# Cosine attention and highway FFN on one core: k and v on 112 lanes of four tokens, transposes by DMA from batch 2 on, v cast by its load, GpSimd behind VectorE's port

## The chip, the core and the metric

One core of a Trainium2 chip runs the whole kernel. The metric is the device time of one execution in microseconds (us); the time before is the median of 3 runs, 313.31 us (312.57 to 313.74). One further execution was profiled. Engines: PE is TensorE (matmuls; PEld are its weight loads), DVE is VectorE, ACT is ScalarE, POOL is GpSimd, SP is SyncE, which here only issues DMA transfers. POOL issues transfers too, and only its transfers change the type on the way (float32 to float16).

## The reference

Eight batches, 12 heads, 448 tokens, 64 elements a head; the rows of q and k are brought to length one, the scores are scaled by 1/tau = 10, and a highway FFN of 768 columns follows.

```python
q_n = q / (np.linalg.norm(q, axis=-1, keepdims=True) + 1e-06)
k_n = k / (np.linalg.norm(k, axis=-1, keepdims=True) + 1e-06)
scores = np.matmul(q_n, k_n.transpose(0, 1, 3, 2)) / tau
attn = np.exp(scores - np.max(scores, axis=-1, keepdims=True))
out  = np.matmul(attn / (np.sum(attn, axis=-1, keepdims=True) + 1e-09), v)
x = out.transpose(0, 2, 1, 3).reshape(B * S, H * D)
H = np.maximum(x @ w_h, 0.0)
T = 1.0 / (1.0 + np.exp(-(x @ w_t + b_t)))
return T * H + (1.0 - T) * x
```

## The kernel before

The heads of a batch are taken in six pairs (head p with head p + 6); pair number s = 6 b + p runs from 0 to 47. 448 tokens are not a multiple of 128: 384 of them lie on 128 lanes with three tokens each ("main"), and the last 64 are "tails" with tiles of their own. Most work is in float16.

For each batch b: main rows of q and k come by POOL's queue as float16 (`qr`, `kr`), v by SP's as float32 (`vr`), tails by SP's (`qt`, `kt`, `vt`). DVE squares the main rows (L462), ACT the tails (L486); DVE folds the squares in two halvings and a sum (L477 to L479), and seven Newton steps of 24 to 48 elements give the reciprocal roots (L505 to L512). A chain of loads, squares, folds and Newton steps thus precedes a batch; its loads of q, k and v wait for an exponential of pair 6 b - 8 (`GO`). Tails of k are scaled by DVE (`ktnorm`, L558).

For each pair:

- POOL scales q and k by their roots (`scaled`, L531; `qtn` for q's tails, L544).
- `turn`: nine PE transposes (L576 to L584) put q, k and tails into one PSUM bank, and DVE copies it to `qT` (L590, 1024 columns).
- `scores`: six matmuls on half of the rows (L599, two for each of three chunks of 128 keys), one full matmul for the 64 tail keys of both heads (`qkt`, L613); ACT takes the exponentials (L606 for a chunk, L618 for the tails).
- ACT casts v into `vp` (L626, and L634 for the tails; DVE does it in batch 0). `vp` has a column of ones, so that the sums of the exponentials come out of the same product.
- `attend`: 32 matmuls of 65 columns (L647, L650, L666); DVE takes the reciprocal (L680) and scales into `x` (L683).

The FFN of a batch has four groups, three of 128 x 768 and one of tails: x is transposed (by a DMA on SP's queue in batches 1 to 6, L709; by PE in batches 0 and 7, L715), PE multiplies by both weights in halves (L738, L744, L749), ACT takes tanh (L763), DVE ends with L770, L777 and L781, POOL adds (L787) and SP stores (L797, L795).

Every engine takes its instructions in the order of the program. That order comes from a list of operation numbers, `ORDER`, which is written out in the kernel; `Plan.follow` goes along it with a cost for each operation, gives each tile a buffer of its ring, and sorts by the starts so found. Work of the FFN is thus put by hand between that of the pairs on every engine. In the planner an operation with `port=True` (of POOL, and of DVE from SBUF to SBUF) starts only when the one before it of either engine is over; in the program nothing enforced this.

Of the kernel before, what the change touches and what calls it, by code (L numbers as in the profile page):

```python
# [19 lines left out]
9 8 4 0 12 10 7 6 11 14 2 13 5 3 18 15 22 23 24 250 25 28 26 16 17 27 29 249 30 248 31 40 32 33 247 251 34 35  # L20
36 37 39 38 20 64 252 65 66 253 63 67 19 68 41 69 21 42 70 43 78 74 51 79 76 75 44 45 46 52 77 72 47 53 73 48
54 1 49 55 50 56 86 57 58 59 60 87 61 62 90 105 88 71 259 109 82 124 80 89 81 83 143 128 97 91 84 98 166 95
106 92 85 125 147 107 96 93 144 108 126 94 162 116 127 110 117 112 163 101 111 100 99 272 164 113 255 129 135
130 131 145 132 133 146 102 136 103 114 165 134 154 466 464 104 173 115 137 254 463 148 465 139 260 256 152
155 140 261 149 119 118 257 467 120 262 121 258 153 167 138 122 263 174 469 141 150 123 168 264 271 151 468
171 265 273 172 169 266 156 274 158 170 267 157 275 159 268 176 276 269 175 160 270 161 177 283 178 277 179
285 278 288 180 279 284 287 280 142 281 181 307 282 329 289 182 291 326 217 310 290 199 286 306 200 298 292
218 299 296 325 308 293 344 327 309 297 294 345 328 317 295 311 364 336 346 312 301 383 347 300 318 302 303
363 337 313 304 315 367 305 355 382 314 365 235 183 356 366 316 332 184 333 319 322 320 185 330 386 334 331
374 321 186 323 335 324 349 187 375 340 350 341 681 679 488 338 339 348 471 353 680 188 351 682 192 354 195  # L30
189 342 343 352 193 683 190 194 357 191 360 358 685 236 368 196 372 369 359 470 384 684 373 201 197 361 385
370 475 362 389 476 202 472 198 371 393 477 219 473 394 478 474 390 387 378 377 479 379 388 487 391 207 480
392 489 208 481 203 490 502 482 491 398 397 396 483 395 492 602 484 376 493 485 545 494 486 495 503 209 526
564 496 380 204 497 507 399 499 498 400 583 205 501 210 500 206 381 504 211 212 401 523 505 542 506 514 213
508 522 515 512 225 509 541 524 513 220 560 525 510 221 222 579 511 543 214 517 686 518 519 516 215 544 527
691 531 520 528 223 521 598 533 216 552 692 226 534 693 529 687 553 240 530 694 688 228 532 241 695 561 227
229 224 689 536 231 418 535 242 580 537 538 690 237 599 539 696 540 548 550 723 238 697 703 551 562 435 698
230 549 581 563 546 239 402 232 547 243 233 582 571 403 572 699 554 700 404 556 701 555 244 818 234 405 702
245 742 780 565 569 720 246 566 557 408 558 719 559 570 406 409 739 407 567 410 586 738 568 411 600 716 587
575 717 576 574 757 601 573 588 577 584 414 589 590 578 758 609 412 591 715 422 413 452 610 419 895 704 585  # L40
898 721 415 896 593 705 592 897 594 416 722 595 603 607 596 604 597 428 899 423 706 608 707 605 425 417 606
708 429 709 901 710 424 426 711 430 718 612 712 611 427 613 900 761 614 713 714 436 776 615 616 726 728 919
727 740 777 730 741 729 420 795 437 617 731 439 421 796 442 438 902 440 724 431 441 745 432 725 749 759 903
443 750 433 760 734 746 735 444 733 732 908 747 904 434 743 907 453 748 814 736 737 445 744 909 905 764 454
910 765 906 815 754 753 911 455 752 448 934 751 459 446 912 755 913 756 799 762 634 766 447 763 778 914 449
768 767 797 915 450 779 456 769 798 783 939 781 916 784 771 920 451 618 917 782 921 621 918 773 922 1034 772
935 958 770 923 457 954 774 924 800 775 651 802 801 619 458 931 787 925 806 620 926 933 622 788 460 624 936
623 627 803 625 630 461 807 628 626 977 1113 1112 804 927 932 785 805 638 928 629 955 635 786 929 1114 930 631
1111 808 636 791 1115 632 637 790 789 639 792 462 640 810 793 811 794 816 647 937 633 817 973 956 1117 938 974
819 823 957 820 825 946 992 809 1116 652 826 812 1011 813 947 668 641 824 1119 821 642 822 1136 658 643 993  # L50
644 1123 1015 827 1012 828 830 829 645 831 832 940 944 646 941 653 833 1118 655 654 648 945 975 1120 656 1124
649 976 942 657 961 943 965 994 664 661 962 650 1125 659 1121 966 1126 1122 1030 963 959 964 662 1127 1031 660
949 850 960 948 1128 951 663 978 1129 665 950 979 968 1130 969 666 952 1131 970 953 980 982 1132 995 981 967
984 667 1013 971 1133 985 972 672 983 1014 669 1134 1155 1135 673 1193 1148 670 1212 1231 1147 674 989 867 671
986 987 1250 1149 988 1174 834 675 990 1152 996 991 837 1171 997 1001 998 835 676 1151 1003 1032 1002 677 838
1033 1004 999 1190 678 1018 839 840 1000 1137 843 1019 841 1170 1007 842 836 1008 1189 1005 1150 1006 1020 846
1016 1138 1021 1022 1153 1009 1139 1023 844 1010 1017 1037 1329 1327 1154 854 1038 845 1024 1328 851 1140 1330
847 855 1141 848 1142 1143 1025 856 1144 1027 1331 1145 1039 1146 1035 1208 1040 1026 1041 1028 1172 1332 1209
1029 1042 852 1036 849 1173 1228 857 1333 868 853 1227 858 863 1043 884 859 860 1046 1334 861 1045 862 1158
1156 1159 864 1162 1191 865 1163 1044 1192 1160 1157 869 1047 1048 1246 871 866 1161 1049 1247 1175 870 872  # L60
1176 1164 1335 1166 1167 1339 1352 1165 873 874 1168 880 1177 1340 1179 1169 1181 1178 1210 1341 1336 875 1182
1342 1180 1196 1337 877 1343 1338 1200 1197 878 876 1198 1201 1066 1194 1344 1211 1186 1199 1183 1345 1219 879
1195 1185 1346 1215 881 1184 1216 1351 1204 1203 1205 882 1187 1220 1347 1202 1188 1213 1390 1217 1348 1206
1214 1349 888 1207 883 885 1353 1218 889 1350 1354 1428 886 1363 890 1371 1223 1355 1083 887 1050 1368 1409
1447 1356 1222 1357 1051 1367 1366 1358 1359 1224 1360 1056 1361 1052 1365 1221 1364 1053 891 1225 1229 892
1362 1226 893 1054 1230 1057 1386 1055 894 1059 1058 1387 1232 1236 1233 1248 1062 1238 1405 1249 1237 1369
1060 1370 1424 1239 1067 1100 1466 1061 1544 1234 1547 1063 1253 1235 1068 1064 1257 1070 1254 1546 1073 1543
1258 1255 1069 1251 1545 1256 1406 1241 1240 1076 1252 1425 1243 1065 1242 1077 1244 1549 1245 1071 1078 1074
1072 1259 1548 1075 1260 1261 1079 1084 1568 1388 1080 1372 1556 1389 1443 1376 1373 1262 1378 1081 1263 1407
1264 1379 1085 1408 1377 1265 1087 1462 1082 1086 1374 1393 1551 1375 1088 1444 1090 1394 1380 1383 1463 1381  # L70
1089 1391 1395 1096 1392 1382 1550 1397 1426 1384 1398 1567 1091 1396 1093 1385 1555 1092 1412 1101 1413 1557
1569 1399 1582 1094 1427 1402 1282 1400 1095 1401 1570 1416 1414 1403 1417 1571 1104 1415 1102 1097 1105 1572
1558 1103 1098 1573 1559 1410 1106 1299 1606 1431 1435 1574 1432 1404 1445 1099 1266 1575 1107 1436 1576 1108
1272 1446 1411 1109 1269 1577 1644 1578 1552 1110 1419 1587 1421 1625 1270 1553 1663 1273 1554 1271 1418 1682
1267 1274 1560 1420 1268 1561 1433 1562 1429 1422 1563 1434 1423 1454 1464 1564 1278 1455 1286 1565 1465 1430
1450 1566 1287 1581 1451 1440 1579 1438 1437 1288 1439 1580 1452 1448 1583 1441 1453 1442 1283 1602 1275 1449
1284 1621 1276 1285 1584 1458 1277 1316 1456 1457 1459 1279 1469 1460 1603 1471 1470 1461 1585 1280 1473 1586
1472 1604 1289 1605 1474 1640 1588 1281 1467 1589 1292 1659 1290 1468 1295 1590 1291 1622 1300 1591 1475 1641
1607 1609 1608 1476 1660 1478 1594 1477 1610 1301 1479 1480 1595 1611 1592 1612 1293 1303 1294 1481 1593 1306
1296 1302 1304 1297 1597 1305 1596 1599 1598 1613 1312 1298 1623 1600 1614 1601 1307 1678 1624 1617 1309 1308  # L80
1679 1626 1630 1627 1310 1632 1311 1498 1631 1317 1313 1320 1633 1314 1318 1321 1319 1628 1322 1515 1642 1629
1323 1315 1615 1324 1482 1643 1325 1636 1651 1326 1647 1652 1649 1618 1648 1616 1634 1619 1661 1650 1620 1483
1662 1485 1484 1670 1486 1671 1637 1487 1635 1645 1638 1664 1494 1646 1488 1639 1502 1665 1489 1656 1490 1668
# [150 lines left out]
def kernel(  # L234
# [11 lines left out]
    nc = tc.nc  # L246
# [639 lines left out]
```

## Time and profile before

| what | value |
|---|---|
| median of 3 runs | 313.31 us |
| the profiled execution | 313.04 us |
| its span, first to last instruction | 311.2 us |
| DVE busy | 240.4 us (77%) |
| ACT busy | 205.8 us (66%) |
| POOL busy | 160.9 us (52%) |
| share of DMA engines: SP's queue, POOL's queue | 39.6%, 28.5% |
| granted TensorE clock over the span | 0.987 |
| first turn of pair 12, last product of pair 47 | 81.1 us, 282.5 us |

A busy matmul is not a PE at its peak: matmuls are pipelined, so what one costs is read from the distance between the starts of neighbours. Three stages can be told apart: a start of some 50 us, in which loads and the norms of the first batches set the pace; the middle, in which pairs and FFN groups are mixed on PE; and a tail of 28.7 us after the last pair, in which only the FFN is left.

### The profile page before, as it was taken

To read this page: it belongs to the slowest core of one execution; us is meant where nothing else is said; L and a number is where in the kernel's file an instruction comes from. 1 tells how busy PE (TensorE), PEld (TensorE's weight loads), DVE (VectorE), ACT (ScalarE), POOL (GpSimd) and SP (SyncE) were. 2 spreads that over 40 slices of the span, in tenths; PEclk is the share of its full clock that TensorE was granted. 3 is DMA by queue.
4 is the path that set the end of the run, shared out by engine and by line. 5 is a ranking of instruction groups with operands and counts; after the bars stand their busy time and mean duration, and the time that the engine had idled before them with its cause. 6 is when DMAs were issued, how large, how long until landed. Compare 5 with 4: busy or idle time off the path is not lost.

```text
span 311.2 us, 7957 instructions
## 1 busy us (share of the span) xinstructions
PE 264.0 (85%) x3178; PEld 164.1 (53%) x3178; DVE 240.4 (77%) x548; ACT 205.8 (66%) x327; POOL 160.9 (52%) x162
## 2 busy tenths in 40 slices
PE   0148946998699999899988999979899999999992
PEld 0115635665356565457555565645565656666661
DVE  5897796489789896998799887994799845454574
ACT  1445972989485868875776949948688795761210
POOL 9539145612882958259456864268712766112440
PEclk9999995999999999999999999999999999999999
DMA  7999999992212399439972399319985014301313
GB/s 170 225 223 216 229 192 240 142 235 88 26 53 51 103 148 280 96 97 154 284 117 78 54 197 285 91 35 138 243 183 103 15 53 101 103 15 54 128 53 126
DMA packets 79750, 42.21 MB, mean 136 GB/s; under 512 B 60224, under 2 KB 76608, under 8 KB 79712
## 3 DMA queue, kind: packets, MB, share of 16 engines
q1 hardware_dynamic: 53104, 29.60, 39.6%
q0 software_dynamic: 24992, 11.31, 28.5%
q10 hardware_dynamic: 1616, 0.79, 0.9%
q8 instruction: 25, 0.41, 0.6%
q14 instruction: 13, 0.11, 0.1%
HBM read 37.75 MB, written 11.01 MB: 157 GB/s over the span
## 4 chain that ended last, share of the span: by engine, by line
PE 43%; DVE 33%; DMA 15%; issue 4%; POOL 2%; ACT 1%; ACTq 0%; DVEq 0%; POOLq 0%
PE pB L749 16%; DMA qr<-in_q_dram 7%; PE pS L599 6%; PE pB L650 5%; DVE f L477 4%; DMA out_dram<-os 4%; DVE n L479 3%; DVE hm L770 3%; DVE x L683 3%; DVE qT L590 3%; DVE sq L462 3%; DMA kr<-in_k_dram 2%; PE pB L744 2%; DVE kb L558 2%; DVE rs L508 2%
## 5 line engine op out<-in xcount | busy, mean ns | idle before, releaser
L606 ACT ACTIVATE E<-pS 128x896 f16<-128x896 f32 x144 | 126.6, 928 | 34.8 <-PE pS L599 34.3
L787 POOL TENSOR_TENSOR os<-x,hm 128x768 f32<-128x768 f16 (+1 forms) x30 | 45.9, 1531 | 90.6 <-DVE hm L781 83.0
L749 PEld LDWEIGHTS <-xT 128*128 128x128 f16 x576 | 51.8, 97 | 43.0 <-issue 16.2
L749 PE MATMUL pB<-wh,xT 128*128 128x384 f16 x288 | 58.7, 327 | 3.5 <-DVE x L683 3.1
L749 PE MATMUL pB<-wt,xT 128*128 128x384 f16 x288 | 61.6, 327 | 0.0
L531 POOL TENSOR_TENSOR qn<-qr,rs 128x384 f16<-128x384 f16 x45 | 41.0, 923 | 18.8 <-DVE rs L512 9.0
L650 PE MATMUL pB<-vp,E 128*128 128x65 f16 x864 | 49.0, 196 | 1.5 <-DVE vp L626 1.4
L763 ACT ACTIVATE tt<-pB 128x384 f16<-128x384 f32 x56 | 27.8, 500 | 30.6 <-PE pB L749 21.5
L599 PE MATMUL pS<-qT 64*128 64x448 f16 x288 | 44.5, 367 | 2.5 <-ACT E L606 2.0
L647 PE MATMUL pB<-vp,Et 128*128 128x65 f16 x288 | 43.3, 195 | 2.2 <-DVE hm L770 2.2
L650 PEld LDWEIGHTS <-E 128*128 128x128 f16 x864 | 40.0, 99 | 7.5 <-issue 3.8
L770 DVE SCALAR_TENSOR_TENSOR hm<-pB,x 128x384 f16<-128x384 f32 x56 | 30.6, 550 | 16.6 <-PE pB L749 13.4
L531 POOL TENSOR_TENSOR kp<-kr,rs 128x384 f16<-128x384 f16 x45 | 42.0, 946 | 2.2 <-PE pB L584 2.2
L590 DVE COPY qT<-pB 128x1024 f16<-128x1024 f16 x48 | 32.4, 684 | 10.8 <-PE pB L584 10.7
L618 ACT ACTIVATE Et<-pB 128x512 f16<-128x512 f32 x48 | 28.5, 603 | 18.3 <-PE pB L613 18.2
L647 PEld LDWEIGHTS <-Et 128*128 128x128 f16 x288 | 28.4, 98 | 7.7 <-issue 5.3
L683 DVE SCALAR_TENSOR_TENSOR x<-pB,rd 128x448 f16<-128x448 f32 x48 | 29.7, 618 | 0.8
L680 DVE RECIPROCAL rd<-pB 128x7 f32<-128x7 f32 x48 | 9.5, 198 | 18.6 <-PE pB L650 12.1
L599 PEld LDWEIGHTS <-qT 64*128 64x128 f16 x288 | 10.5, 95 | 22.4 <-issue 17.9
L613 PE MATMUL pB<-qT 128*128 128x512 f16 x48 | 18.8, 399 | 3.0 <-DVE qT L590 2.4
L544 POOL TENSOR_TENSOR qtn<-qt,rs 128x384 f16<-128x384 f32 x8 | 8.1, 1009 | 24.6 <-DVE rs L512 24.6
L777 DVE TENSOR_SCALAR tt<-tt 128x768 f16<-128x768 f16 (+1 forms) x32 | 15.8, 497 | 6.0 <-ACT tt L763 5.9
(73 smaller groups left out, 443.7 us busy)
## 6 DMA issues: line engine op xcount, KB each, us to landing
vr<-in_v_dram SPq DMA_DIRECT2D x8, 1152.0 KB, 11.7
out_dram<-os SPq DMA_DIRECT2D x24, 384.0 KB, 2.8
kr<-in_k_dram POOLq DMA_DIRECT2D x7, 576.0 KB, 13.8
qr<-in_q_dram POOLq DMA_DIRECT2D x7, 576.0 KB, 11.1
vt<-in_v_dram SPq DMA_DIRECT2D x16, 96.0 KB, 7.8
out_dram<-os SPq DMA_DIRECT2D x16, 96.0 KB, 2.2
qt<-in_q_dram SPq DMA_DIRECT2D x30, 48.0 KB, 5.3
kt<-in_k_dram SPq DMA_DIRECT2D x14, 96.0 KB, 5.8
```

The lines of the kernel that those rows point to most:

```text
L531: e.tensor_mul(R("qn" if t == 0 else "kp", s).rearrange("l c ab d -> l ab c d"), rows(t, b, p, p + 1)[:, :, 0, :].rearrange("l ab (c d) -> ...
L590: op("DVE", f"cpT {s}", lambda: nc.vector.tensor_copy(R("qT", s)[:, :], R16(("T", ti))[:, :]), o, l, key, r=[("B", ("T", ti))], w=[("qT", s)])
L599: nc.tensor.matmul(R("S", 3 * s + c)[:, ab, 0:448], lhsT=qT[:, 512 + 128 * c : 640 + 128 * c], rhs=qT[:, 64 * (1 - ab) : 64 * (1 - ab) + 4 ...
L606: nc.scalar.activation(R("E", s)[:, c, :, 0:448], R("S", 3 * s + c)[:, :, 0:448], AF.Exp, scale=inv_tau)
L618: op("ACT", f"exp {s} t", lambda: nc.scalar.activation(R("Et", s)[:, 64:576], R("B", ("S", s))[:, :], AF.Exp, scale=inv_tau), o, l, key + 0.3,
L647: nc.tensor.matmul(U[:, 2 * c + ab, :], lhsT=Et[:, 128 + 128 * c : 256 + 128 * c], rhs=vp[:, 6 + ab, :], start=True, stop=False)
L650: nc.tensor.matmul(U[:, 2 * c + ab, :], lhsT=EF[:, j, 576 * ab + 128 * c : 576 * ab + 128 * c + 128], rhs=vp[:, 3 * ab + j, :], start=Fals ...
L683: op("DVE", f"ev {s}", lambda: nc.vector.scalar_tensor_tensor(out=R("x", b)[:, :, D * p : D * p + D], in0=U_()[:, :, 0:D], scalar=0.0, in1 ...
L749: nc.tensor.matmul(P[:, 0:MH], lhsT=xT[:, cc, :], rhs=w_[:, cc, MH * mh : MH * mh + MH], start=st, stop=(cc == CC - 1))
L763: op("ACT", f"th {g} {mh}", lambda pi=pi, mh=mh: nc.scalar.activation(R("tt", g)[:, MH * mh : MH * mh + MH], R("B", ("P", pi))[:, 0:MH], A ...
L770: nc.vector.scalar_tensor_tensor(out=R("hm", g)[:, MH * mh : MH * mh + MH], in0=R("B", ("P", pi))[:, 0:MH], scalar=0.0, in1=xs, op0=ALU.ma ...
L787: op(en, f"out {g}", lambda: eng.tensor_add(R("os", g)[:, 0:W], xall(), R("hm", g)[:, 0:W]), o, l, at + 0.1, r=[("gg", g), ("x", b)], w=[( ...
```

## The change

k and v lie on 112 lanes of four tokens, so that they have no tails; q stays on 128 lanes of three with its 64 tail tokens (now dealt to lanes by even and odd heads). The scaled q and k of a pair stand side by side in one tile `N` of seven blocks of 128 x 128. In batches 0 and 1 eight PE transposes turn them; from batch 2 on (`DT = 2`) one transposing DMA on SP's queue turns all seven blocks of a pair straight into `qT`, one more for each batch turns q's tails (`qtT`), and DVE copies 64 columns of these to `qT` for each pair. `ktnorm`, the tails of v and the tail matmul are gone; the scores have four chunks of three matmuls (384, 448 and 64 columns). v comes by POOL's queue as float16. The tails of q come in two transfers for a batch instead of four. Lanes 96 to 127 of some tiles are set once to constants (before lanes up to 111 are written), since 16 lanes of k hold nothing. Of the planner only the list is left: order and buffers (`ORDER`, `SLOTS`) are written out, both new, so that work moves on all engines. POOL operations with `port=True` get a wait for the last DVE operation with `port=True` that stands before them (`after`).

```diff
+    KL, KC = 112, 4
+    PG = 6 + 2 * KC
     def main_src(t, b):
-        return t[b, :, 0 : 3 * 128, :].rearrange("h (l c) d -> l h (c d)", c=NCH)
+        if t is q:
+            return q[b, :, 0 : 3 * 128, :].rearrange("h (l c) d -> l h (c d)", c=NCH)
+        return t[b].rearrange("h (l c) d -> l h (c d)", c=KC)
...
     def load_v(b, key, gate=()):
-        def fv():
-            nc.sync.dma_start(R("vr", b)[:, :, :], main_src(v, b))
-        def ft():
-            for ab in range(2):
-                nc.sync.dma_start(R("vt", b)[64 * ab : 64 * ab + 64, :, :], tail_src(v, b, ab))
+        load_main("vr", v, b, 0, 6, key, gate)
...
     def scaled(t, b, p, key, eng):
-            e.tensor_mul(
-                R("qn" if t == 0 else "kp", s).rearrange("l c ab d -> l ab c d"),
+            dst = R("N", s)[0 : LN[t], 0:NCH] if t == 0 else R("N", s)[0 : LN[t], NCH:]
+            return e.tensor_mul(
+                dst.rearrange("l c ab d -> l ab c d"),
...
-    def ktnorm(b, key):
-        for ab in range(2):
...
+        if b >= DT:
+            op("SP", f"tt {b}", lambda: nc.sync.dma_start(
+                R("qtT", b)[:, :, :], R("qtn", b).rearrange("l i ab d -> l (i ab d)"), transpose=True), 1230, 0, key + 0.1,
+               r=[("qtn", b)], w=[("qtT", b)], dma=(384, 23.5, 1))
...
     def turn(b, p, key):
+        if b >= DT:
+            op("SP", f"td {s}", lambda: nc.sync.dma_start(
+                R("qT", s)[:, 64:].rearrange("d (j l) -> d j l", l=128), R("N", s).rearrange("l j ab d -> l (j ab d)"),
+                transpose=True), 1230, 0, key - 0.5, r=[("Np", s, 0), ("Np", s, 1)], u=[("N", s)], w=[("qT", s)],
+               dma=(128 * (NCH + KC), 23.5, 1))
+            h = 64 * (p % 2)
+            op("DVE", f"cpt {s}", lambda: nc.vector.tensor_copy(R("qT", s)[:, 0:64], R("qtT", b)[:, p // 2, h : h + 64]),
+               90, 200, key - 0.2, r=[("qtT", b)], w=[("qT", s)], port=True)
+            return
...
     def scores(b, p, key):
-        for c in range(NCH):
+        for c in range(KC):
             def fn(c=c):
-                for ab in range(2):
+                for ab, at, lo, hi in ((0, 0, 64, 448), (1, 0, 0, 448), (0, 384, 0, 64)):
                     qT = R("qT", s)[64 * ab : 64 * ab + 64]
-                    nc.tensor.matmul(R("S", 3 * s + c)[:, ab, 0:448], lhsT=qT[:, 512 + 128 * c : 640 + 128 * c],
-                                     rhs=qT[:, 64 * (1 - ab) : 64 * (1 - ab) + 448], start=True, stop=True)
+                    nc.tensor.matmul(R("S", KC * s + c)[:, ab, at : at + hi - lo], lhsT=qT[:, 448 + 128 * c : 576 + 128 * c],
+                                     rhs=qT[:, lo:hi], start=True, stop=True)
...
-        def ft():
-            qT = R("qT", s)
-            nc.tensor.matmul(R("B", ("S", s))[:, :], lhsT=qT[:, 896:1024], rhs=qT[:, 0:512], start=True, stop=True)
...
     def attend(b, p, key):
-                nc.tensor.matmul(U[:, 2 * c + ab, :], lhsT=Et[:, 128 + 128 * c : 256 + 128 * c],
-                                 rhs=vp[:, 6 + ab, :], start=True, stop=False)
-                for j in range(NCH):
+                for j in range(KC):
+                    nc.tensor.matmul(U[:, 2 * c + ab, :], lhsT=E[:, j, 576 * ab + 128 * c : 576 * ab + 128 * c + 128],
+                                     rhs=vp[:, KC * ab + j, :], start=(j == 0), stop=(j == KC - 1))
...
+    def after(ins, on):
+        tc.add_manual_dep(ins.ins, on.ins.name, mybir.DependencyInfo(
+            mybir.DependencyClass.Sync, mybir.DependencyReason.SCHED_ONLY), reason="shared port")
-    plan = pl.follow(ORDER)
+    plan = pl.follow(ORDER, SLOTS)
+    last = None
     with nc.allow_low_precision(reason="fp16 operands of the products, squares and gates as given"):
         with tc.manual_schedule():
             for o in plan:
-                o.fn()
+                ins = o.fn()
+                if o.port and o.eng == "DVE":
+                    last = ins
+                elif o.port and last is not None:
+                    after(ins, last)
```

## The prediction, made before the changed kernel had run

> **What bounds the kernel now.** I read the page first, then the busy times of the stretch from 81 to 283 us (pairs 12 to 47, the ones that the DMA transposes will serve), then the timelines of PE, DVE and POOL inside it, then the transposes on SP's queue. From the page and from that stretch:
>
> ```profile
> PE 264.0 (85%) x3178; PEld 164.1 (53%) x3178; DVE 240.4 (77%) x548; ACT 205.8 (66%) x327; POOL 160.9 (52%) x162
> ```
>
> ```profile
> 81.00:283.00 202.00, 190.30 (x2355) 117.50 (x2354) 159.64 (x346) 149.80 (x237) 112.08 (x106) 1.00 0.62 121
> ```
>
> The second line has PE, PE's loads, DVE, ACT, POOL, clock, DMA share and GB/s. PE is idle for 202.0 - 190.3 = 11.7 us of 202 at full clock: it sets the pace of the middle, 202 / 36 = 5.6 us a pair. What a turn costs it is read from starts, since ends are pipelined:
>
> ```profile
> 130.10 0.22 PE L576 MATMUL pB<-swap,qtn 128*128 128x128 f16 x1 [0.48 <-DVE x L683]
> 130.16 0.33 PE L578 MATMUL pB<-ident,qn 128*128 128x128 f16 x3
> 130.32 0.22 PE L580 MATMUL pB<-swap,qtn 128*128 128x128 f16 x1
> 130.38 0.33 PE L582 MATMUL pB<-ident,kp 128*128 128x128 f16 x3
> 130.54 0.22 PE L584 MATMUL pB<-ident,kb 128*128 128x128 f16 x1
> 130.69 0.68 PE L744 MATMUL pB<-wh,xT 128*64 128x384 f16 x6
> 131.88 0.55 PE L599 MATMUL pS<-qT 64*128 64x448 f16 x4 [0.51 <-DVE qT L590]
> 132.37 0.20 PE L647 MATMUL pB<-vp,Et 128*128 128x65 f16 x1
> ```
>
> Nine transposes from 130.10 to 130.69, 0.59 us; the turn before it, from 128.73 to 129.24, took 0.51. Four score matmuls take 131.88 to 132.37, 0.245 us a chunk.
>
> A second limit is close behind, and no share of busy time names it. POOL, then DVE, at one place:
>
> ```profile
> 20.68 0.82 POOL L531 TENSOR_TENSOR qn<-f,rs 128x384 f16<-128x384 f32 x1 [5.10 <-DVE rs L512]
> 21.47 0.82 POOL L531 TENSOR_TENSOR kp<-f,rs 128x384 f16<-128x384 f32 x1
> 22.25 0.82 POOL L531 TENSOR_TENSOR qn<-f,rs 128x384 f16<-128x384 f32 x1
> ```
>
> ```profile
> 20.75 0.81 DVE L508 TENSOR_TENSOR rs<-rs 128x36 f32<-128x36 f32 x1
> 21.59 0.76 DVE L510 SCALAR_TENSOR_TENSOR rs<-rs,n 128x36 f32<-128x36 f32 x1
> 22.38 0.75 DVE L512 SCALAR_TENSOR_TENSOR rs<-rs 128x36 f32<-128x36 f32 x1
> 23.16 0.20 DVE L508 TENSOR_TENSOR rs<-rs 128x36 f32<-128x36 f32 x1
> ```
>
> The same Newton step takes 0.20 us alone and 0.81 while POOL works: it ends some 60 ns after POOL's operation does (20.68 + 0.82 = 21.50; 21.56). DVE from SBUF and POOL exclude each other; DVE reading PSUM does not wait (the `qT` copy of L590 stays within 642 to 693 ns).
>
> **The change part by part.** The sum is made against the profiled execution, 313.04 us: span 311.2 and 1.84 around it. It lies 0.3 us below the median of 313.31.
>
> *Turns on PE.* 36 of the 48 go. At 0.51 to 0.59 us each that is 18.4 to 21.2 us, all on the path as long as PE paces; I take 0.55, **-19.8**. The eight transposes of pairs 0 to 11 instead of nine are 12 x 0.055, nothing.
>
> *Scores.* Before, a pair takes 3 x 0.245 and one matmul of 512 columns (0.22 us, by the 0.163 us from start to start of 384 columns, L749), 0.95 us. After, four chunks with as many columns as before in each half of the rows, but three matmuls. Lower bound 4 x 0.245 = 0.98; upper bound with 0.055 more in each chunk (a small matmul's pitch, as in the turn) 1.20. The short one can run beside the other half, so I take 1.05: 48 x 0.10 = **+5** (bounds +1 and +12). `attend` keeps 32 matmuls (0.032 us each by L647 and L650); fewer rows change no start.
>
> *DVE.* Gone are 36 copies of 0.683 us (24.6 us) and 16 of L558 (13.2 us). New are 36 copies of 64 columns, between 0.1 and 0.25 us by the smallest rows (L508: 0.198 median). Squares of k grow by a third (0.75 to 1.0 us, 15 of them), folds by 42/36. DVE is 79% busy in the stretch and the net is a loss of work, so nothing is charged there.
>
> *ACT.* Four exponentials of 896 columns for three and one of 512: in the stretch L606 takes 95.2 us and L618 21.2, so +31.7 - 21.2; the casts of v grow by some 3.5, the tails' casts (5.2) and squares of k's tails (2.6) go. 149.8 becomes about 156 of some 187 us: hidden, unless PE's time fell by a further 30.
>
> *POOL and the shared path.* Alone, a scaling of 384 takes 0.825 us (minimum 822 and 819, L531), an add of 768 takes 1.637 and of 384 0.906 (L787). The 69 scalings, 5 of L544, 18 and 6 adds of the stretch make 96 us; DVE's from-SBUF work there at its undisturbed durations (L462 0.75, L477 0.745, L478 0.45, L505 to L512 0.2, L558 0.55, L777 0.31, L781 0.55) makes 69. Together 165 of 202 us, 82%. After, k's scaling of 512 costs about 1.1 us (between 0.83 and 1.64), so POOL has 106.5; DVE with larger squares and folds, 36 small copies and without L558 has 72: 178.5 us. PE after has 202 - 19.8 + 3.8 = 186 us for the same pairs. If each short DVE step costs only the 60 ns that it needs behind POOL, 100 Newton steps give back 14 us and 164 remain. So the shared path fits, at 88 to 96%, without much air.
>
> The new waits put POOL behind DVE's last port operation in program order: behind it are the scalings of the next pairs, their transposes on SP and then PE. Before, POOL could begin early and the chip made it wait anyway, so a wait is worth nothing where both meet, and a loss only where DVE is late itself (its L781 behind L770 behind PE). Bounds: -5 (fewer collisions) to +16 (the 82% of now stays the ceiling, below). I take **+2**, near the case in which it fits.
>
> [...]
>
> *Transposes on SP.* The nearest rows are the existing ones, of six blocks:
>
> ```profile
> L709 SPq DMA_TRANSPOSE xT<-x x24: 1188/1217/6171, 82.4 to 277.4; - x24
> ...
> DMA to landing us min/median/max: 2.3/2.8/10.2
> ```
>
> Seven blocks: 2.8 us, or some 3.0, in quiet. Behind loads the issue alone took 3.36 (at 186.75) and 3.66 us (at 222.68), so 5.0 to 5.3 in all; the maximum of 10.2 came behind v on the same queue, and v leaves it. SP issues for a batch six at 1.22, one for `qtT`, four for x, two for q's tails and five stores: under 18 of some 31 us. What matters is the lead. Counted in the written order for pairs 25 and 26, during a load: from the FFN half that POOL's add of group 7 needs, PE has 20 FFN halves (0.5 us each and five biases), 16 chunks of scores and 16 groups of eight products before pair 25, about 19 us. POOL's part up to k of pair 25 takes 13 us, the transpose 2.8 to 5.3: 0.8 to 3.3 us of air. For pair 26 it is 0.5 to 3. So nothing is charged, with little to spare; a late one stops PE, since PE takes its order as written.
>
> *v on POOL's queue.* Seven more issues at 1.05 us in the middle and start (L366), on an engine 55% busy: hidden, except where the air above is used.
>
> [...]
>
> *Start.* L558 (two of 0.83 us on the first chain, at 11.88) goes; loads come in fewer and larger packets; PE's wait for x of 5.5 us before the first PE transposes of x, after which one slice of 7.8 us shows the clock at half, may shrink. Bounds 0 to -9; I take **-4**. The tail of 28.7 us is FFN alone and stays.
>
> Sum: -19.8 + 5 + 2 - 4 = -16.8, so 296 us.
>
> **The rivals.**
>
> *Better: PE's idle goes too (285).* DVE loses 38 us of copies, and of PE's 11.7 us of idle time in the stretch many waits name DVE (L683, L590, L770). If 11 us in all vanish besides, 285. Against: the coupling takes DVE's place.
>
> *Eaten by late transposes (309, between 300 and 316).* 12 us of each 33 are load time, so 13 of 36 pairs turn in it. If POOL runs behind so that the air above is gone, each loses about 1 us and the next ones some of it: 13 us. For it: air of 0.5 us at the low end. Against: the buffers (`N` and `qT`, four each) let transposes run two to three pairs ahead.
>
> *Slower: lockstep on the shared path (325).* POOL waits for DVE, DVE for PE, PE for the transposed pair that POOL has not scaled. If DVE and POOL together cannot fill more than the 82% of now, the stretch takes 178.5 / 0.82 = 217.7 us, 15.7 more than 202: 313.0 + 15.7 - 4 = 325. It decides as soon as they cannot pass 178.5 / 202 = 88%. For it: POOL's work grows by 10 us while the pace shortens. Against: 82% was seen while PE was the limit, not they, and POOL then stood for 62 us waiting for L781.
>
> **How the numbers follow.** Forecast 0.55, better 0.15, eaten 0.15, lockstep 0.15. A measurement of this kernel tells about 0.5% (1.6 us) from no change. The forecast and the better case are faster; of the eaten case 0.09 is faster and 0.06 within 0.5%; lockstep is slower: 0.79, 0.06, 0.15. The forecast's own range is 288 to 305 (scores +1 to +12, start 0 to -9, not all at one end). Below 285 lies about half of the better case, above 314 most of the lockstep, so 285 to 314 leaves out 2 in 10.
>
> **What would show it.** PE busy in the middle down by some 15 us, and its idle time still near 12; L512 and its fellows no longer at 0.75 where POOL works; transposes of `qT` landing in 3 us, in 5 during loads. Wrong would be: PE standing in front of score matmuls for the DMA of `qT` (late transposes), or POOL's idle time ending at DVE's L777, L781 and Newton steps with PE's idle above 25 us (lockstep), or score chunks above 0.3 us.

## The result and the profile after

The changed kernel takes 324.85 us (median of 4 runs, 322.75 to 327.32) against 313.52 us before in the same session: ratio 1.037, 95% interval 1.032 to 1.043. It is 3.7% slower. The profiled execution took 325.69 us, its span is 323.6 us. Times below are medians of those executions of a kernel that lie within 1.5% of its fastest; the profiled executions of e3_mixed (315.45 us) and g4_mixed_no_waits (322.42 us) lie outside.

From the page of the changed kernel, the busy times, then PE's busy tenths and its granted clock in 40 slices of 8.1 us:

```profile
PE 264.0 (82%) x3082; PEld 157.4 (49%) x3082; DVE 203.0 (63%) x522; ACT 215.7 (67%) x303; POOL 165.2 (51%) x168
...
PE   0048788999669977997699957999489999999993
...
PEclk9999997999959997999599997999969999999999
```

PE executes 96 matmuls fewer and is busy for as long as before, and its share falls from 85% to 82%. Every fourth or fifth slice of the middle has a hole in PE, and the clock has one at the same place or just behind it. Before, the middle had no hole in the clock (granted 1.00 from 81 to 283 us; now 0.94 from 81 to 294). The holes come once a batch. DVE's busy time fell by 37 us. Where PE and ACT wait now is told by the list of waits (engine and line, what it waited for, us in all, times, longest):

```profile
PEld L544 <- DMA qT<-N: 20.3, 8, 5.4
POOL os L707 <- DVE hm L701: 19.6, 8, 7.3
...
PE pS L544 <- DMA qT<-N: 18.0, 6, 5.1
ACT sqt L436 <- DMA qt<-in_q_dram: 16.9, 5, 7.9
```

`POOL os <- DVE hm` was 83.0 us before; it is 19.6. PE and its loads wait for `qT<-N`, the new DMA transposes, and ACT waits for q's tails. One of these waits, on PE's timeline (start, duration, engine, line; in brackets the idle time before):

```profile
85.73 0.66 PE L669 MATMUL pB<-wh,xT 128*128 128x384 f16 x3
91.45 0.55 PE L544 MATMUL pS<-qT 64*128 64x384 f16 x3 [5.06 <-DMA qT<-N]
```

and the queue that should have delivered, SP's, around the same time:

```profile
70.94 1.30 SPq L358 DMA_DIRECT2D qt<-in_q_dram  x2
72.40 9.40 SPq L513 DMA_TRANSPOSE qT<-N  x3
81.89 0.54 SPq L717 DMA_DIRECT2D out_dram<-os  x1
82.54 3.57 SPq L629 DMA_TRANSPOSE xT<-x  x1
86.34 0.64 SPq L717 DMA_DIRECT2D out_dram<-os  x1
```

The line of L513 holds three transposes, of pairs 13, 15 and 14, issued at 72.40, 77.69 and 79.06 us. They landed 9.2, 10.0 and 12.4 us after their issue; the last one landed at 91.41 us, and PE went on at 91.45. (In the written order pair 15's transpose stands ahead of pair 14's, which PE needs first; the other order was not tried.) POOL had issued the loads of k, q and v of batch 3 at 72.3, 73.3 and 75.6 us; they landed between 81.9 and 94.0. Over all 36 transposes of pairs the line of L513 says:

```profile
L513 SPq DMA_TRANSPOSE qT<-N x36: 1221/1256/3578, 69.6 to 272.6; - x36
...
DMA to landing us min/median/max: 2.9/3.6/13.8
```

Six stalls of PE between 86 and 236 us (5.06, 4.12, 4.69, 5.48, 2.46 and 2.93 us) make 24.7 us. Four of them (16.8 us) end with a transposed pair, like the one shown. Those of 5.48 and 2.46 us end with ACT, which had stood 7.88 and 5.07 us for q's tails; the first of these on ACT's timeline:

```profile
194.74 0.52 ACT L436 ACTIVATE sqt<-qt 128x384 f16<-128x384 f32 x1 [7.88 <-DMA qt<-in_q_dram]
```

Compared by pairs, from the first score matmul of pair 18 to the last product of pair 47: 165.7 us before (116.8 to 282.5), 178.6 us after (115.2 to 293.8). Up to pair 11 the two kernels are within 1 us (first scores at 70.4 and 69.4 us), and the FFN behind the last pair takes 28.7 and 29.8 us. The loss lies in the middle.

### The profile page after: what moved, and what is told of

Its sections match the earlier page's. It is cut to its first block, busy times and chain, and to the rows that moved or that the text cites. A ratio compares the mean times of both kernels' runs of the same rounds, so it can differ in the third digit from the quotient of the medians.

```text
span 323.6 us, 7705 instructions
## 1 busy us (share of the span) xinstructions
PE 264.0 (82%) x3082; PEld 157.4 (49%) x3082; DVE 203.0 (63%) x522; ACT 215.7 (67%) x303; POOL 165.2 (51%) x168
## 5 line engine op out<-in xcount | busy, mean ns | idle before, releaser
L552 ACT ACTIVATE E<-pS 112x896 f16<-112x896 f32 x192 | 166.1, 920 | 50.2 <-PE pS L544 46.4
L544 PE MATMUL pS<-qT 64*128 64x448 f16 (+2 forms) x576 | 66.9, 308 | 30.6 <-DMA qT<-N 18.0
L707 POOL TENSOR_TENSOR os<-x,hm 128x768 f32<-128x768 f16 (+1 forms) x30 | 44.0, 1469 | 69.2 <-DVE hm L701 19.6
L577 PE MATMUL pB<-vp,E 112*128 112x65 f16 x1152 | 58.6, 201 | 0.9 <-ACT E L552 0.9
L480 POOL TENSOR_TENSOR N<-kr,rs 112x512 f16<-112x512 f16 x45 | 47.4, 1060 | 22.6 <-DVE f L429 5.5
L577 PEld LDWEIGHTS <-E 112*128 112x128 f16 x1152 | 48.6, 103 | 17.5 <-issue 13.1
L544 PEld LDWEIGHTS <-qT 64*128 64x128 f16 x576 | 24.8, 96 | 65.0 <-issue 33.0
L480 POOL TENSOR_TENSOR N<-qr,rs 128x384 f16<-128x384 f16 x45 | 37.4, 839 | 34.8 <-issue 12.0
L564 ACT COPY vp<-vr 112x512 f16<-112x512 f16 x42 | 24.4, 631 | 0.6 <-DMA vr<-in_v_dram 0.6
L586 PE MATMUL pB<-vp,E 112*128 112x65 f16 x384 | 21.2, 198 | 0.0
L701 DVE TENSOR_TENSOR hm<-tt,hm 128x768 f16<-128x768 f16 (+1 forms) x32 | 18.9, 591 | 0.5
L586 PEld LDWEIGHTS <-E 112*128 112x128 f16 x384 | 16.5, 101 | 5.0 <-issue 3.8
L658 PE MATMUL pB<-bth,ones 128*128 128x384 f16 x48 | 15.9, 331 | 2.5 <-ACT tt L683 2.5
## 6 DMA issues: line engine op xcount, KB each, us to landing
wh<-in_moe_w_h_dram POOLq DMA_DIRECT2D x1, 1152.0 KB, 12.4
```

The costliest lines, as they stand in the source:

```text
L480: return e.tensor_mul(dst.rearrange("l c ab d -> l ab c d"), rows(t, b, p, p + 1)[:, :, 0, :].rearrange("l ab (c d) -> l ab c d", c=n), rc ...
L544: nc.tensor.matmul(R("S", KC * s + c)[:, ab, at : at + hi - lo], lhsT=qT[:, 448 + 128 * c : 576 + 128 * c], rhs=qT[:, lo:hi], start=True, ...
L552: nc.scalar.activation(R("E", s)[0:KL, c, :, 0:448], R("S", KC * s + c)[0:KL, :, 0:448], AF.Exp, scale=inv_tau)
L564: return nc.vector.tensor_copy(dst, src) if ondve else nc.scalar.copy(dst, src)
L577: nc.tensor.matmul(U[:, 2 * c + ab, :], lhsT=E[:, j, 576 * ab + 128 * c : 576 * ab + 128 * c + 128], rhs=vp[:, KC * ab + j, :], start=(j = ...
L586: nc.tensor.matmul(U[:, 6, :], lhsT=E[:, j, 384 + 64 * ab : 512 + 64 * ab], rhs=vp[:, KC * ab + j, :], start=(n == 0), stop=(n == 7))
```

## The experiments

Theory 1: the DMA transposes, and q's tails on the same queue, come late because they run beside the loads of a batch, and PE, which takes its order as written, stands for them. Theory 2: lockstep on the path that POOL and DVE share (in the kernel before, a Newton step of 0.20 us took 0.81 beside POOL, and a scaling of 0.83 us up to 1.35 beside DVE's squares), kept by POOL's new waits, which was the slower one of the prediction's rivals and gave the right time, 325 us.

| run | what | us (median) | ratio to before, 95% |
|---|---|---|---|
| changed kernel | | 324.85 | 1.037 (1.032 to 1.043) |
| e1_no_waits | without POOL's waits | 334.78 | 1.068 (1.062 to 1.074) |
| e2_thin_loads | one head of twelve loaded in batches 4 to 7 | 297.63 | 0.950 (0.947 to 0.954) |
| e3_mixed | 16 of the 36 pairs turned on PE | 312.48 | 0.996 (0.991 to 1.001) |
| e4_all_pe | all pairs turned on PE | 311.64 | 0.995 (0.992 to 0.998) |
| f1_before_waits | kernel before, with the waits | 311.15 | 0.993 (0.988 to 0.998) |
| f2_tails | q's tails loaded early | 321.04 | 1.028 (1.019 to 1.038) |
| f3_mixed_tails | e3 and f2 together | 299.76 | 0.957 (0.949 to 0.965) |
| f4_warm | matmuls in place of standing | 324.90 | 1.037 (1.027 to 1.047) |
| g1_few_tails | f3 with 10 pairs on PE | 303.36 | 0.966 (0.959 to 0.973) |
| g2_spread | f2, loads of a batch apart | 322.34 | 1.027 (1.018 to 1.036) |
| g3_mixed_spread | f3, loads of a batch apart | 309.01 | 0.986 (0.980 to 0.992) |
| g4_mixed_no_waits | f3 without POOL's waits | 317.94 | 1.014 (1.008 to 1.019) |

### The waits of POOL alone (e1_no_waits)

```diff
                 ins = o.fn()
-                if o.port and o.eng == "DVE":
-                    last = ins
-                elif o.port and last is not None:
-                    after(ins, last)
```

> GpSimd's waits for VectorE's last port operation are taken away, all else as in the changed kernel. Theory 1 (the DMA transposes of qT, and with them q's tails on the same queue, come 9 to 14 us after their issue while a batch's loads run; PE stands for them and then runs at half clock for some us): the five gaps of PE of 2.5 to 5.5 us between 86 and 236 us stay, time 320 to 327 us. Theory 2 (lockstep: POOL waits for DVE, DVE for PE, PE for a pair that POOL has not scaled): the gaps shrink, 313 us or less.

334.78 us, slower by 9.9 us than the changed kernel: neither theory had that. The stalls for `qT<-N` stayed (17.6 us on PE), and taking the waits away did not help, so a lockstep that the waits keep falls. Whether the shared path sets the pace even without them is left to the next run, which keeps all work on it. DVE's busy time rose from 203.0 to 232.7 us. The waits are worth something; g4 below says what.

### The loads thinned (e2_thin_loads)

```diff
-                nc.gpsimd.dma_start(d, s)
+                m = 1 if b >= 4 else 12
+                nc.gpsimd.dma_start(d[:, 0:m, :], s[:, 0:m, :])
```

> In batches 4 to 7 the loads of q, k and v bring one head of twelve, so five sixths and more of their rows are never loaded and the output is not the reference's; every instruction and wait stays. The loads of batch 3 (around 72 us) stay whole, as the control. Theory 1 (transposes late behind the loads): the transposes of the pairs from 18 on land in 3 to 4 us, the last four gaps of PE with their halved clock go (some 17 us of standing and 20 us at half clock, which costs half of it), the first one at 86 us stays: 296 to 303 us. Theory 2 (lockstep on the shared path): nothing of POOL's, DVE's and PE's work has changed, 319 us or more.

297.63 us: 27.2 us less than the changed kernel, with all of its instructions and waits. The work of POOL and DVE is all there, so theory 2, which needed 319 us or more, is ruled out, and it is the loads that cost these 27 us. The transposes landed within 2.9 to 5.2 us from pair 18 on; those of pairs 13 to 15, which stand behind the load of batch 3 that stayed whole, took 9.7 to 12.3 us as before, and the one stall left is theirs, 4.90 us at 85 us. The row of the thinned kernel for the stretch behind that (us, then PE, PE's loads, DVE, ACT, POOL, clock, DMA share, GB/s):

```profile
103.00:266.00 163.00, 161.62 (x2003) 95.93 (x2001) 110.00 (x289) 139.69 (x198) 95.01 (x97) 1.00 0.62 121
```

PE is idle for 1.4 of 163 us at full clock. Pairs 18 to 47 take 151.6 us (113.8 to 265.4), 14.1 less than before the change and 27.0 less than after it. The rows that were never loaded also came sooner to DVE and ACT, so this run doesn't say how the 27 us divide between transposes and squares; the next ones go further.

### Part of the pairs, or all, back on PE (e3_mixed, e4_all_pe)

Here `turn` takes its old form for the pairs in `PET`, with its place in the written order:

```diff
     DT = 2
+    PET = (13, 14, 15, 19, 20, 21, 24, 25, 26, 27, 31, 32, 33, 37, 38, 39)
...
-        if b >= DT:
+        if b >= DT and s not in PET:
             op("SP", f"td {s}", lambda: nc.sync.dma_start(
```

> The 16 pairs whose transposes fall into a load window (13 to 15, 19 to 21, 24 to 27, 31 to 33, 37 to 39) are turned on PE as before the change, eight transposes of 0.055 us and a copy of 960 columns each; the other 20 keep their DMA transpose. Theory 1: no stall of PE of 4 us and no half clock in the middle, 16 turns of 0.5 us given back to PE: 298 to 308 us. Theory 2 (lockstep; DVE gets 16 copies of 0.65 us more): 319 us or more.

> All pairs are turned on PE; of the change there stay the 112 lanes of k and v without tails, v cast by its load, and the waits of GpSimd (the transposes of q's tails into qtT are still issued, unused). Theory 1: no stall of 4 us, all 36 turns (18 to 20 us) back on PE: 305 to 318 us, so about what the kernel before takes. Theory 2 (lockstep): DVE's 36 copies come back too, 319 to 330 us, with POOL's idle time ending at DVE's Newton steps.

With all pairs on PE the stalls are gone (the longest idle time of the middle is 0.82 us) and the time is 311.64 us, in the range of theory 1: without DMA transposes of pairs the rest of the change is about even with the kernel before. The mixed kernel missed its range, 312.48 us. It kept two stalls of 5.25 and 4.91 us. The first one ends with ACT, whose timeline has the cause:

```profile
179.36 0.52 ACT L437 ACTIVATE sqt<-qt 128x384 f16<-128x384 f32 x1 [7.65 <-DMA qt<-in_q_dram]
179.79 0.90 ACT L553 ACTIVATE E<-pS 112x896 f16<-112x896 f32 x1
180.58 0.61 ACT L565 COPY vp<-vr 112x512 f16<-112x512 f16 x1
```

ACT, in order, stood 7.65 us for q's tails. Their load was issued at 167.8 and 169.8 us together with the batch's loads, and its second half took 9.4 us. In e4, where SP's queue carries no transposes of pairs, the same loads of the last three batches took 2.6 to 3.0 us; those of batch 4, issued 1.4 and 2.1 us behind the load of k, took 8.5 and 9.2 even there. The second stall is a late transpose again:

```profile
215.75 0.56 PE L545 MATMUL pS<-qT 64*128 64x384 f16 x3 [4.91 <-DMA qT<-N]
```

It is that of pair 36, which was not among the 16: issued at 207.47 us, just as the loads of the last batch began, it took 8.2 us.

### q's tails loaded early (f2_tails, f3_mixed_tails)

The loads of `qt` for batches 3 to 7 move up in the written order, between two load windows (a load window is the time in which the loads of a batch run); their ring has two buffers, and the one they take is free by then.

```diff
-            load_tails(b, base - 9 if b > 1 else -10, gate)
+            load_tails(b, base - 9 if b > 1 else -10)
```

> The changed kernel; the loads of q's tails for batches 3 to 7 stand some 100 to 200 instructions earlier in the written order, between two load windows, all else as it was. Theory 1: ACT's waits for these tails (16.9 us in five, the longest 7.9) go, and with them the stalls of PE at 190.6 and 229 us with their half clock; the three that end with a late transposed pair stay: 312 to 319 us. Theory 2 (lockstep on the shared path): 322 us or more.

> 16 pairs turned on PE as in the run before this one, and the loads of q's tails moved as in this call's second run. Theory 1: the two stalls of 5.25 and 4.91 us that the mixed kernel kept (ACT's square stood 7.7 us for q's tail) go with their half clock, 13 us: 298 to 306 us. If the mixed kernel's remaining time is set by something else (VectorE's copies, the shared path), 309 us or more.

In the changed kernel it brought 3.8 us, less than expected, and the intervals of the two ratios overlap: ACT's wait fell from 16.9 to 1.8 us, but the transposes behind the loads were late all the same, and PE's waits for `qT<-N` rose from 18.0 to 21.2 us in its place. In the mixed kernel it brought 12.7 us: 299.76 us, 4.3% faster than the kernel before and the fastest version that loads all of its data. Pair 36's transpose, too, now takes 3.0 us; this one edit took both stalls away, and the runs don't divide the gain between them. From its page, and for its transposes:

```profile
PE 263.2 (88%) x3210; PEld 162.1 (54%) x3210; DVE 211.0 (71%) x522; ACT 216.4 (72%) x303; POOL 164.3 (55%) x168
...
PEclk9999899799999999999999999999999999999999
```

```profile
L514 SPq DMA_TRANSPOSE qT<-N x20: 1221/1248/2114, 70.1 to 247.5; - x20
...
  PE pS L545: 2.4, 4
...
DMA to landing us min/median/max: 2.9/3.0/4.6
```

No transpose takes over 4.6 us, the clock has no hole in the middle (1.00 from 74 to 270 us), and PE's longest idle time there is 0.85 us. The two causes of late data lay behind each other: against the changed kernel the mixed turns alone brought 12.4 us, the tails alone 3.8, both together 25.1.

### Is the halved clock a cost of its own? (f4_warm)

```diff
+    for s, n in ((14, 18), (19, 18), (24, 18), (30, 18), (37, 12)):
+        def warm(s=s, n=n):
+            for i in range(n):
+                nc.tensor.matmul(R("S", 97)[:, 0, :] if s == 24 else R("B", ("W", s))[:, :],
+                                 lhsT=ident[:, :], rhs=wh[:, 0, 0:512], start=True, stop=True)
+        op("PE", f"warm {s}", warm, 220 * n, 220 * n, 0, mode="F", ...)
```

> The changed kernel with 12 to 18 matmuls of 512 columns (0.22 us each, results unused) on PE right ahead of each of the five score matmuls that stood for 2.9 to 5.5 us: work in place of standing, which no later instruction needs. If the halved clock behind each stall is a cost of its own, the clock stays at full speed through the stalls, and the time falls by up to half of the 28 us of half clock: 311 to 318 us. If the half clock only fell where PE had to wait anyway, or does not come from the standing: 322 to 330 us.

The clock did stay up; from the page of this run:

```profile
PEclk9999799999999999999799999999799999999998
```

In the middle the periods at half clock fell from 27.3 us to 6.8 us, and the time did not: 324.90 us. That is what the second case of the expectation said. In the trace of the changed kernel a period at half clock, of 3.4 or 6.8 us, lies around or behind each of its stalls of 4.1 to 5.5 us; what a stall must last for it is not shown. Keeping the clock up this way brought nothing that can be measured here. By estimate the 84 extra matmuls cover some 18.5 us (at 0.22 each; ten of them take 2.32 us on this run's timeline), and 9.3 us of stalls remained at or near the old places, 27.8 us together against 24.7 before. That PE's lost time is set by when the data come, and that the saved half-clock time went into other waits, is a reading of these sums; as the extra matmuls take PE's time themselves, the run does not price the fall of the clock alone.

### How much one load window carries (g1_few_tails, g2_spread, g3_mixed_spread)

```diff
-    PET = (13, 14, 15, 19, 20, 21, 24, 25, 26, 27, 31, 32, 33, 37, 38, 39)
+    PET = (14, 15, 19, 20, 25, 26, 31, 32, 37, 38)
```

That is g1, against f3. In g2 and g3 the loads of k and q of batches 3 to 7 stand 140 and 70 places earlier in the written order, which alone is changed.

> The mixed kernel with q's tails loaded early, but only 10 pairs turned on PE (14, 15, 19, 20, 25, 26, 31, 32, 37, 38), where it had 16. If the six pairs given back to DMA transposes land in time, 6 x 0.5 us come off: 295 to 299 us. If two DMA transposes in one load window already make each other late (three or more transfers of the queue at about 4 us each beside the loads), stalls of PE of 2 us and more come back: 302 to 312 us.

> All pairs from batch 2 on by DMA transpose, q's tails early, and the loads of k and q of batches 3 to 7 issued some 140 and 70 places of the written order sooner (about 22 and 11 us), v's as it was, so that the three loads of a batch run one after the other instead of together. If the transposes are late because several of them meet one long window of loads, the landings shrink to some 4 to 7 us and the stalls to under 2 us each: 295 to 308 us. If any load beside a transpose is enough, the total of load time being the same, the stalls stay: 315 to 324 us.

> The mixed kernel (16 pairs on PE) with q's tails early, and the loads of k and q spread as in the run before. VectorE stood for k and q (8 us in all) and would not any more: 295 to 300 us. If the 20 DMA transposes, which stood outside the load windows, now meet loads, and PE stands for them: 302 to 312 us.

Six more pairs by DMA made it 3.6 us slower, not 3 us faster; a stall of 2.69 us at 140 us came back, and PE's waits for `qT<-N` were 6.1 us for 2.4. Spreading the loads helped neither kernel: g2 is even with f2 (322.34 us from two executions, against 321.04), g3 lost 9.3 us against f3. The median landing of a transpose rose from 4.0 us in f2 to 5.5 us in g2, and PE's waits in g2 are as long in all as in f2 (21.2 us in eight), only more of them:

```profile
PEld L544 <- DMA qT<-N: 24.2, 12, 6.1
...
PE pS L544 <- DMA qT<-N: 20.6, 10, 6.0
```

By these numbers the loads that lay together left quiet time for transposes between them; spread out, they met more of them. What helped was to keep transposes out of the load windows (f3, 299.76 us, against 321.04 for f2).

### What the waits are worth without late transposes (g4_mixed_no_waits)

The edit of e1 in the kernel f3:

```diff
-                if o.port and o.eng == "DVE":
-                    last = ins
-                elif o.port and last is not None:
-                    after(ins, last)
```

> The mixed kernel with q's tails early, without GpSimd's waits for VectorE. Theory A (the waits are worth 10 us by themselves, since the order puts VectorE's port steps together ahead of POOL's): VectorE's busy time 235 to 245 us instead of 211, time 306 to 312 us. Theory B (the waits only kept the late transposes of the changed kernel from being later): within 1 us of the 299.8 us with them.

317.94 us for 299.76: the waits are worth 18.2 us here, more than theory A gave them, and theory B falls. DVE's busy time is 238.0 us for 211.0. Its timeline, then POOL's, near 50 us of the run without waits:

```profile
49.36 7.83 DVE L412 TENSOR_TENSOR sq<-qr 128x1152 f16<-128x1152 f16 x1
57.11 0.95 DVE L412 TENSOR_TENSOR sq<-kr 112x1536 f16<-112x1536 f16 x1
57.98 0.64 DVE L535 COPY qT<-pB 128x960 f16<-128x960 f16 x1
```

```profile
49.37 2.05 POOL L481 TENSOR_TENSOR N<-kr,rs 112x512 f16<-112x512 f16 x2
51.38 1.61 POOL L481 TENSOR_TENSOR N<-qr,rs 128x384 f16<-128x384 f16 x2
52.96 1.03 POOL L481 TENSOR_TENSOR N<-kr,rs 112x512 f16<-112x512 f16 x1
53.96 1.60 POOL L481 TENSOR_TENSOR N<-qr,rs 128x384 f16<-128x384 f16 x2
55.53 1.03 POOL L481 TENSOR_TENSOR N<-kr,rs 112x512 f16<-112x512 f16 x1
```

A square that takes 0.75 us (its median in both runs) stood through eight scalings in a row and ended 0.6 us behind the last of them; behind it on DVE stood the copy of `qT`, and PE idled 6.02 us for that. With the waits, the same square of f3 started at 47.44 and took 0.75 us, and POOL began at 51.32. In e1 the square at this place took 5.25 us; the next square, of k, stands behind it:

```profile
50.51 5.25 DVE L411 TENSOR_TENSOR sq<-qr 128x1152 f16<-128x1152 f16 x1
55.67 1.58 DVE L411 TENSOR_TENSOR sq<-kr 112x1536 f16<-112x1536 f16 x1
```

POOL's scalings ran there from 50.52 to 57.94 us without a break. The first square ended 0.6 us behind the fifth of them, while the sixth ran; the second one ended 0.8 us behind the sixth, while the seventh ran. Read from these times, DVE was let in while POOL's row still went on, here after five instructions and after one; the other squares of q that met POOL in g4 took 1.3 to 1.9 us. Both squares that stood through many had started some 10 ns ahead of POOL's first one. What decides it is not shown.

### The waits in the kernel before (f1_before_waits)

The same waits, and Newton's steps marked as port operations, in the kernel before. Every engine keeps its order; some tiles get another buffer.

```diff
             for o in plan:
-                o.fn()
+                ins = o.fn()
+                if o.port and o.eng == "DVE":
+                    last = ins
+                elif o.port and last is not None:
+                    after(ins, last)
```

> The kernel before, and of the change only GpSimd's waits for VectorE's last port operation; nothing else is altered. Taking the waits away from the changed kernel cost it 10 us and gave VectorE 30 us more busy time. Theory A (the waits save collisions wherever the two engines share the path): here too VectorE's busy time falls by 25 to 35 us from 240, and the time to 303 to 310 us. Theory B (the waits helped only in an order that was planned with them; in an order that was not, they make POOL late): 316 to 330 us.

311.15 us, 0.7% faster: between the ranges of the two theories. DVE's busy time hardly fell, from 240.4 to 237.2 us (15 Newton steps of the three kinds above 0.5 us where there were 20, of 102; the changed kernel has none). A wait holds POOL back for what DVE has ahead of it in the order; it doesn't hold DVE back from starting while POOL works. In the changed kernel the wait ends most collisions (DVE is busy for 203.0 us, and for 232.7 without it); that this is because DVE's port steps stand together ahead of POOL's in its order is argued, not tried.

## Why the prediction was wrong

It gave 296 us (285 to 314) and 0.79 to faster; the kernel takes 324.85 us.

**The step that failed: "Seven blocks: 2.8 us, or some 3.0, in quiet. Behind loads ... 5.0 to 5.3 in all", "So nothing is charged".** In quiet they take 2.9 to 3.0 us, as said. Beside loads ten of the 36 took 9.1 to 13.8 us, and where the sum charged nothing, PE stood for 24.7 us. Four things went wrong in it. First, the price was reckoned from how long the issue took, not from the landing. The trace of the kernel before has the landings of the two transposes of x that the prediction names, at 186.75 and 222.68 us (the last number of each line):

```profile
xT<-x SPq DMA_TRANSPOSE x1, 8.4
...
xT<-x SPq DMA_TRANSPOSE x1, 7.3
```

So they took 8.4 and 7.3 us with six blocks, not 5.0 to 5.3 with seven. Second, the maximum of that row, 10.2 us, was set aside because "v leaves" SP's queue; but with v on POOL's queue a transpose took up to 13.8 us. Counted from the packet records of the changed kernel, SP's queue moved 775 packets a microsecond alone (71 to 72 us) and 237 and 247 beside the loads (78 to 80 us), while POOL's queue moved 240 and 250 in the same time; in bytes both together moved 183 GB/s, no more than SP's queue alone before (191). A transpose of a pair is 928 packets (SP's queue has 33,408 fewer when the 36 are gone), so, as an estimate from these counts, 1.2 us of packets in quiet and 3.8 beside loads. Third, "under 18 of some 31 us" added up the queue's issue times in quiet; it left out that what the queue carries in a load window takes, by that estimate, three times as long and stands in line: two loads of tails, three transposes of pairs, the stores and a transpose of x meet in the window from 71 us. Fourth, lateness was priced at 1 us a pair in the rival, but SP issued pair 14's transpose 7.3 us ahead of PE's need, and it took 12.4.

From 78 to 80 us the two queues thus moved nearly equal numbers of packets, SP's of 256 bytes and POOL's mostly of 512. Why they share the time like this is not shown; the landings of 8.4 and 7.3 us in the trace of the kernel before were there to be read.

**The other terms, and some luck.**

- *Turns, -19.8.* Right in size: from start to start a turn took 0.53 us before in the stretch of pairs 18 to 47.
- *Scores, +5.* By the distances of starts 1.01 us a pair before and 1.09 in the thinned kernel: +4.
- *`attend`, nothing.* "Fewer rows change no start" did not hold: a product takes 37 ns from start to start in the thinned kernel for 34 before, about 0.1 us a pair, by estimate 4 to 5 us in all.
- *PE's idle time, left as it was.* For pairs 18 to 47 the thinned kernel takes 14.1 us less than before, and the prediction's 0.55 - 0.10 us a pair make 13.5 for 30. The agreement is partly luck: PE is busy for 150.2 us there where it was 157.2, so half of the 14.1 us is idle time that went (8.5 us before, 1.4 after).
- *ACT and POOL.* Forecast 156 and 106.5 us of busy time for pairs 12 to 47; the stretch from 81 to 294 us has 153.4 and 108.1.
- *Port, +2.* No run measures this net against the kernel before. Its reason was wrong: "a wait is worth nothing where both meet". Without the waits this order loses 9.9 us (e1), or 18.2 (g4), where the bound on the side of a gain was 5.
- *v on POOL's queue, hidden.* It wasn't tried by itself what v's load, now issued by the same engine 2 to 3 us behind k's and q's, adds to the load window.
- *Start, -4; tail, unchanged.* -0.9 and +1.1.

The thinned kernel's 297.63 us lies near the 296 of the sum, but it kept one stall of 4.90 us, gained less at the start, and lost the idle time that the sum had kept. The forecast was that of a kernel whose transposes are on time; that the figures meet so closely is in part chance.

**The rivals.** "Eaten by late transposes" had the mechanism and half of its price: 13 us (1 us for each of 13 pairs) against 27 by e2. "Lockstep on the shared path" had the time, 325 us, and the wrong mechanism, and its signs alone would not have told: PE's idle time in the stretch from 81 to 294 us is 26.4 us, above the 25 named, and POOL's waits that end at DVE are 108 us in all for 123 before, though the add's own fell from 83.0 to 19.6. What tells is what PE waits for, that taking POOL's waits away made things worse, and that with the loads thinned the same work on the path fits into 297.63 us. The first sign in the prediction's list of what would be wrong, PE in front of score matmuls for the DMA of `qT`, is the one that came.

## What to carry to other kernels

A DMA that replaces engine work must be priced by its landing, not its issue, beside the traffic of its own stretch and with everything that its queue carries in that window: here v's load had moved to another queue, and ten of 36 transposes still took 9.1 to 13.8 us beside loads, for 2.9 to 3.0 in quiet. Loads came in bursts here, and it paid to use the DMA transposes between the bursts and the engine within them. Look for the next late transfer behind the one just repaired. And a rival that gives the right time proves nothing: look at its waits in the profile, and take its cause away in a run.

## What was not expected of the hardware

- A DVE operation that met POOL on their shared path could stand through many of POOL's instructions: a square of 0.75 us took 7.83 us beside eight of them in g4, and 5.25 us beside five in e1. The other squares of q that met POOL in g4 took 1.3 to 1.9 us, and the Newton steps of the prediction's row, 0.75 to 0.81 us for 0.20, ended behind one instruction each. Why those two squares stood for so long is not shown.
- Beside loads with packets of mostly 512 bytes, SP's queue of 256-byte packets fell from 775 to some 240 packets a microsecond (changed kernel, 71 to 72 and 78 to 80 us).
- PE's granted clock was at half for 3.4 to 6.8 us around or behind each long stall, 27.3 us in all in the changed kernel; f4 brought that down to 6.8 us, and the time stayed (324.90 us for 324.85).
